# One pool of eight PSUM banks for scores and everything else, with an own buffer for Q staging, in a transformer layer on one core

## The chip, the cores and the metric

The kernel runs on one core of one Trainium2 chip. Times are device microseconds (us) of whole executions; a profile is one further execution that the hardware profiler recorded. PE is TensorE's matmuls, PEld its weight loads, ACT ScalarE, DVE VectorE, SPq the queue from which SyncE issues DMAs.

## The reference

In short: the kernel computes one pre-normalised transformer layer on 2048 tokens of width 1024: attention with 32 query heads of width 32 that share one key and one value head, then a gated feed-forward block (FFN) of width 3584.

```python
x_norm = layernorm(x)
q = (x_norm @ wq).reshape(B, S, 32, 32)      # 32 heads
k, v = x_norm @ wk, x_norm @ wv              # one shared head
p = softmax(q k^T / sqrt(32))                # 32 x 2048 x 2048 exponentials
h = x + (p v) @ wo
h2 = h + (sigmoid(hn @ w_gate) * (hn @ w_up)) @ w_down     # hn = layernorm(h)
```

All inputs are bf16.

## The kernel before

The kernel is written out by a planner of its own. While the program is built, a list scheduler with assumed costs walks along TensorE's time and decides, step by step, which piece of work PE does next; the order on every engine is fixed then, and the chip runs it in that order with semaphores.

The work comes in groups. A score group (S) is 16 row-tiled matmuls (each on 32 of the 128 rows, `32*128` in the views) that fill four PSUM banks; there are 512 of them, and ACT turns each into probabilities with exponentials. A PV group multiplies probabilities with V. OP is the output projection, GU a gate/up pair of the FFN, D the down projection, Q the query projection. The FFN runs in passes: tokens 0 to 127, then 128 to 255, then 256 tokens at a time. While there is little real work at the start, PE runs warm-up fillers, matmuls whose results nobody uses. In the views, QTb and kT are Q and K transposed, Pr the probabilities, Vaug V with one more column, OT the attention output transposed and wo_sb its weights, hnT the normalised h transposed, ring the gate and up weights, hact the gated product and zone other large operands.

PSUM has eight banks. Before, six belong to the scores (three units of two neighbouring banks, so one exponential always covers 1024 columns), and two to all other groups. Only one of the other groups is open at a time:

```python
S_ps = psum_tensor("S_ps", [P, 6, 512], F32)       # scores only
F_ps = psum_tensor("F_ps", [P, 2, 512], F32)       # everything else
qst  = hact[:, :]                                  # Q staging lives in hact
...
# planner, one turn
if can_s and run - t < 750.0:        # ACT would soon run dry: scores first
    emit_S(v)
elif cur is not None:                # go on with the one open group
    ...
else:                                # open the next group, by priority
    banks = [b for b in range(2) if known(bank_rel[b], t)]
    # xT, KV, Q0, PV, OP, D, GU, Q
```

The product `hact` of the first FFN pass waits until the last Q staging has been stored (`deps += q_store[-NQS:]`), because Q staging and `hact` share memory, and this pass may start only when all Q groups are done (`q_left[0] == 0`).

The softmax here doesn't subtract the row's maximum and nothing guards it: scores larger than these inputs give would overflow.

## Time and profile before

| | before |
|---|---|
| median of the first runs | 1199.36 us |
| profiled span | 1196.8 us |
| PE busy | 1169.7 us, 98% |
| ACT busy | 1043.8 us, 87% |

From the page of the kernel before: the span, the busy times of the engines, and the clock that TensorE was granted in 40 slices of the span (9 is 90% or more of full speed).

```profile
span 1196.8 us, 47622 instructions
PE 1169.7 (98%) x22204; PEld 830.8 (69%) x22204; DVE 293.6 (25%) x799; ACT 1043.8 (87%) x1312; POOL 38.5 (3%) x84
PEclk9999989999999999999999999999999999999999
```

PE looks saturated, but matmuls are pipelined and their ends are modelled in the profile, so a busy PE is not PE at its peak. From the starts of successive instructions, PE needs about 1150 us for this list of work, so some 42 us are waiting or half clock. The next view sums the waits of PE by what ended them: the total in us, the number of waits, the longest.

```profile
PE S_ps L349 <- ACT Pr L548: 7.3, 10, 1.4
PE F_ps L349 <- issue: 6.8, 8, 2.1
PE S_ps L349 <- issue: 3.5, 4, 1.8
...
PE F_ps L349 <- DVE hact L699: 0.7, 1, 0.7
PE F_ps L349 <- ACT Pr L548: 0.6, 1, 0.6
```

"issue" is a wait for which the profile shows no releaser. The group lines say what an exponential and the output projection cost (busy us, mean ns of one, then the idle time of the engine before them).

```profile
L548 ACT ACTIVATE Pr<-S_ps 128x1024 bf16<-128x1024 f32 x1024 | 977.5, 1042 | 28.5 <-PE S_ps L349 27.7
L349 PE MATMUL F_ps<-wo_sb,OT 128*128 128x512 bf16 x256 | 65.0, 384 | 0.6 <-issue 0.6
```

The clearest single stall stands in the timeline from 146 to 153 us (start, length, instruction, count; in brackets the idle time before it and its releaser).

```profile
146.72 7.53 ACT L548 ACTIVATE Pr<-S_ps 128x1024 bf16<-128x1024 f32 x8
...
147.88 0.40 PE L349 MATMUL S_ps<-QTb,kT 32*128 32x128 bf16 x16 [1.40 <-ACT Pr L548]
149.72 0.61 PE L349 MATMUL S_ps<-QTb,kT 32*128 32x128 bf16 x16 [1.43 <-ACT Pr L548]
151.55 0.61 PE L349 MATMUL S_ps<-QTb,kT 32*128 32x128 bf16 x16 [1.22 <-ACT Pr L548]
152.54 0.48 DVE L699 SCALAR_TENSOR_TENSOR hact<-tnh,F_ps 128x128 bf16<-128x128 f32 x2 [8.08 <-ACT Pr L548]
...
152.88 1.28 PE L349 MATMUL F_ps<-Vaug,Pr 128*128 128x33 bf16 x39 [0.72 <-DVE hact L699]
```

DVE idles 8.08 us: its product cannot be written into `hact`. Both F banks therefore stay full, PE has only score groups, and these come at ACT's pace. PE's four waits here add to 4.8 us. Half clock follows for 6.8 us.

### The profile page before, as it was taken

The page shows a single profiled execution, that of the slowest core. Times are in us where ns is not written, and L with a number is a line of the kernel's source. Part 1 is how long each engine was busy: PE and PEld are TensorE (multiplying, and loading weights), DVE is VectorE, ACT ScalarE, POOL GpSimd, SP SyncE. Part 2 cuts the span into 40 slices and gives each one's busy share as a digit, 9 for nine tenths or more (in the row PEclk, how much of TensorE's full clock was granted, in tenths as well). Part 3 has the DMA queues.
Part 4 walks back from the last instruction along what each step waited for, and adds up shares of the span by engine and source line. Part 5 has one row for each costly group of instructions (what it writes and reads, how often), then busy time and mean ns, then how long its engine had stood idle before and what let it go on. Part 6 is the DMA issues. An engine that isn't in the chain of part 4 may idle for free.

```text
span 1196.8 us, 47622 instructions
## 1 busy us (share of the span) xinstructions
PE 1169.7 (98%) x22204; PEld 830.8 (69%) x22204; DVE 293.6 (25%) x799; ACT 1043.8 (87%) x1312; POOL 38.5 (3%) x84
## 2 busy tenths in 40 slices
PE   9999988999999999999999999999999999999999
PEld 5755567677577856787577856777568765786684
DVE  8423212121213121221212221213122221222121
ACT  6899989999999999999999999999999999981120
POOL 4100000000000000000000000000000000000000
PEclk9999989999999999999999999999999999999999
DMA  8665499489456632667155650666226750479480
GB/s 241 161 182 155 138 280 242 107 210 286 82 142 160 178 90 55 163 177 182 29 122 151 194 118 12 159 178 178 64 64 178 187 139 15 117 192 228 123 208 18
DMA packets 332021, 176.74 MB, mean 148 GB/s; under 512 B 52016, under 2 KB 322352, under 8 KB 331824
## 3 DMA queue, kind: packets, MB, share of 16 engines
q1 hardware_dynamic: 329744, 173.57, 55.6%
q8 instruction: 174, 2.85, 1.0%
q10 hardware_dynamic: 2080, 0.13, 0.1%
q14 instruction: 23, 0.19, 0.0%
HBM read 155.32 MB, written 7.34 MB: 136 GB/s over the span
## 4 chain that ended last, share of the span: by engine, by line
PE 88%; ACT 6%; issue 2%; DVE 2%; DMA 2%; SPq 0%; ACTq 0%; DVEq 0%
PE F_ps L349 75%; PE S_ps L349 13%; ACT Pr L548 5%; DMA q_scratch<-hact 1%; ACT tnh L692 1%; DVE st L290 0%; DMA ring<-in_A_x_dram 0%; DVE st L292 0%; DMA zone<-ring 0%; DVE ring L329 0%; ACT ring L333 0%; DVE hact L699 0%; DVE ring L336 0%; ACT zone L236 0%; DVE mv L294 0%
## 5 line engine op out<-in xcount | busy, mean ns | idle before, releaser
L548 ACT ACTIVATE Pr<-S_ps 128x1024 bf16<-128x1024 f32 x1024 | 977.5, 1042 | 28.5 <-PE S_ps L349 27.7
L349 PE MATMUL F_ps<-hnT,ring 128*128 128x256 bf16 (+1 forms) x4032 | 446.9, 263 | 5.1 <-issue 4.2
L349 PEld LDWEIGHTS F_ps<-hnT,ring 128*128 128x128 bf16 x4032 | 342.6, 98 | 62.9 <-issue 8.9
L349 PEld LDWEIGHTS F_ps<-Vaug,Pr 128*128 128x128 bf16 x8192 | 229.2, 96 | 29.1 <-issue 3.7
L349 PE MATMUL F_ps<-Vaug,Pr 128*128 128x33 bf16 x8192 | 244.2, 177 | 3.7 <-issue 1.9
L349 PE MATMUL S_ps<-QTb,kT 32*128 32x128 bf16 x8192 | 208.4, 218 | 11.0 <-ACT Pr L548 7.3
L349 PE MATMUL F_ps<-zone,hact 128*128 128x512 bf16 x896 | 213.7, 380 | 0.0
L349 PEld LDWEIGHTS S_ps<-QTb,kT 32*128 32x128 bf16 x8192 | 119.3, 93 | 124.2 <-ACT Pr L548 73.7
L699 DVE SCALAR_TENSOR_TENSOR hact<-tnh,F_ps 128x256 bf16<-128x256 f32 (+1 forms) x252 | 97.7, 391 | 439.5 <-ACT tnh L692 431.3
L692 ACT ACTIVATE tnh<-F_ps 128x256 f32<-128x256 f32 (+1 forms) x252 | 93.9, 378 | 86.2 <-PE F_ps L349 86.2
L349 PEld LDWEIGHTS F_ps<-zone,hact 128*128 128x128 bf16 x896 | 78.8, 98 | 88.0
L349 PE MATMUL F_ps<-zone 128*128 128x256 bf16 (+2 forms) x512 | 75.4, 289 | 2.0 <-ACT QTb L236 1.4
L731 DVE SCALAR_TENSOR_TENSOR h_sb<-F_ps,h_sb 128x512 bf16<-128x512 f32 x32 | 22.1, 691 | 204.7 <-PE F_ps L349 204.7
L349 PE MATMUL F_ps<-wo_sb,OT 128*128 128x512 bf16 x256 | 65.0, 384 | 0.6 <-issue 0.6
L581 DVE RECIPROCAL rL<-F_ps 128x4 f32<-128x4 f32 x128 | 23.3, 182 | 140.1 <-PE F_ps L349 140.0
L349 PEld LDWEIGHTS F_ps<-zone 128*128 128x128 bf16 x512 | 37.3, 97 | 23.7 <-ACT QTb L236 1.6
L304 POOL TENSOR_SCALAR zb<-mvb 128x1 bf16<-128x1 bf16 (+1 forms) x25 | 5.6, 225 | 1046.9 <-DVE mvb L300 1046.9
L583 DVE TENSOR_TENSOR Osb<-F_ps,rL 128x128 bf16<-128x128 f32 x128 | 37.3, 291 | 4.2
L349 PEld LDWEIGHTS F_ps<-wo_sb,OT 128*128 128x128 bf16 x256 | 22.1, 99 | 23.0 <-issue 1.9
L625 DVE TENSOR_TENSOR h_sb<-F_ps,xres 128x512 bf16<-128x512 f32 x32 | 22.1, 691 | 47.2 <-PE F_ps L349 47.2
L237 DVE CAST hact<-F_ps 128x512 bf16<-128x512 f32 x24 | 16.6, 691 | 38.2 <-PE F_ps L349 38.1
L349 PE MATMUL S_ps<-hact,ident 128*128 128x512 bf16 x76 | 19.8, 411 | 1.8 <-POOL ident L242 1.8
(36 smaller groups left out, 154.8 us busy)
## 6 DMA issues: line engine op xcount, KB each, us to landing
ring<-in_B_w_gate_dram SPq DMA_DIRECT2D x126, 512.0 KB, 4.3
ring<-in_B_w_up_dram SPq DMA_DIRECT2D x126, 512.0 KB, 6.0
zone<-in_B_w_down_dram SPq DMA_DIRECT2D x7, 1024.0 KB, 8.5
xres<-in_A_x_dram SPq DMA_DIRECT2D x16, 256.0 KB, 2.8
out_dram<-h_sb SPq DMA_DIRECT2D x32, 128.0 KB, 1.7
q_scratch<-hact SPq DMA_DIRECT2D x24, 128.0 KB, 2.8
QTb<-q_scratch SPq DMA_DIRECT2D x6, 512.0 KB, 5.0
ring<-in_A_x_dram SPq DMA_DIRECT2D x5, 512.0 KB, 6.8
```

What stands on the lines that cost most here:

```text
L237: lambda: DVE.tensor_copy(out=out_ap, in_=in_ap))
L304: f = pl.op("pool", lambda: POOL.tensor_scalar(out=zb[:, ph, sl].unsqueeze(2), in0=mvb[:, ph, sl, 1:2], scalar1=LN_EPS_BF16, scalar2=None, ...
L349: return lambda: PE.matmul(o, lhsT=l, rhs=r, start=start, stop=stop, **kw)
L548: exps[u] = pl.op("act", lambda slot=slot, pb=pb: ACT.activation(out=Pr[:, slot, :].rearrange("p (a b) -> p a b", a=2), in_=S_ps[:, pb:pb ...
L581: a = pl.op("dve", lambda: DVE.reciprocal(rL[:, k, :].unsqueeze(2), ov[:, :, DH:DH + 1]), [last], prio=0, occ=70, lat=280)
L583: e = pl.op("dve", lambda: DVE.tensor_tensor(out=Osb[:, qb % 2, g * P:(g + 1) * P].rearrange("p (a b) -> p a b", a=4), in0=ov[:, :, 0:DH], ...
L625: h_ev[(t, dc)] = pl.op("dve", lambda: DVE.tensor_tensor(out=h_sb[:, t % 4, sl], in0=F_ps[:, b, :], in1=xres[:, t % 2, sl], op=ALU.add), [ ...
L692: a = pl.op("act", lambda: ACT.activation(out=tnh[:, k, 0:n], in_=F_ps[:, b, 0:n], func=ACTF.Tanh, scale=0.5), [last, tn_user.get(k)], pri ...
L699: e = pl.op("dve", lambda: DVE.scalar_tensor_tensor(out=hactT[:, ft, 0:n], in0=tnh[:, k, 0:n], scalar=1.0, in1=F_ps[:, b, 256:256 + n], op ...
L731: e = pl.op("dve", lambda: DVE.scalar_tensor_tensor(out=h_sb[:, t % 4, sl], in0=F_ps[:, b, :], scalar=0.5, in1=h_sb[:, t % 4, sl], op0=ALU ...
```

## The change

The intent: let whichever work needs a bank have one, so that PE has something else to do when one group waits, and take away the memory conflict behind the stall above. The diff, cut to its core:

```diff
-    NB = 3
+    SMAX = 8
+    FMAX = 3
+    NQS = 4
-        xres = SB("xres", [2, D])
+        qst = SB("qst", [NQS, 512])
-        S_ps = EC(nc.psum_tensor("S_ps", [P, 6, 512], F32))
-        F_ps = EC(nc.psum_tensor("F_ps", [P, 2, 512], F32))
+        PS = EC(nc.psum_tensor("PS", [P, 8, 512], F32))
-        qst = hact[:, :].rearrange("p (a b) -> p a b", b=512)
 ... s_plan(): any four free banks serve a score group; neighbours preferred
+                w = 2 if i % 2 == 0 and free[i + 1] == free[i] + 1 else 1   # else two exps of 512
 ... x is loaded into h_sb in place of xres
-                    deps += q_store[-NQS:]
+                    deps += []
-  gr.gate = lambda: s in slab_ld and (q_left[0] == 0 if c == 0 else ...)
+  gr.gate = lambda: s in slab_ld and (True if c == 0 else ...)
 ... planner: two groups may be open
-                if can_s and run - t < 750.0:
+            return max(pl.free["act"], t) + sum(...) - t < 1000.0
+        URGENT = ("xT", "KV", "PV", "OP")
+            if banks and len(active) < 2 and f_use < (FMAX if v else 6):
+            if new is not None and (not go or (new[0] in URGENT and RANK[new[0]] < RANK[go[0][0].cls])):
 ...                                  # an urgent group breaks into the open one
-                                 deps if (kk == 0 and j == 0) else [], occ=15.0, lat=15.0 + 170.0 + SEM)
+                              deps if (r == 0 and j == 0) else [], occ=14.0, lat=14.0 + 200.0 + SEM)
```

So three things change in the pool: before the first scores, up to six banks may hold the other groups; afterwards up to three may; and two such groups may be open, the more urgent breaking in.

## The prediction

> **What bounds it now.** Two engines almost tie: the page gives PE 1169.7 us busy, ACT 1043.8, of 1196.8. Starts of successive instructions in the timeline give what each needs:
>
> - PE: 216 ns per 512-column matmul, 109 per 256, 56 per 128, 25 per 33; a score group of 16 row-tiled matmuls 188 ns, plus about 96 going in and 147 coming out. (The Trainium skill, "TensorEngine Tiling (Array Packing)", Key Properties, says a change of tiling mode drains TensorE; the trace agrees with these gaps.) Summed over the instruction order: about 1150 us.
> - ACT: 906 ns per exp of 1024 columns, 264 per tanh of 256, 157 per tanh of 128: 1007 us.
>
> So about 42 us is PE waiting or slowed, plus 5 us at the ends. Excess over PE's need by stretch: 5 us before 60; 6 in 60 to 150; 10.5 in 150 to 200; 10 in 200 to 300; 7 in 300 to 424; 5 afterwards. After 424 us PE is the limit and hardly waits. From the first scores (27.7 us) to score group 160 (357.7 us) takes 330 us, where ACT needs 302 and PE 296.
>
> The clearest stall is 146 to 153 us: the timeline shows DVE waiting 8.1 us at the first gated product (its hact is the Q staging, still being stored), both F banks stuck, only score groups left, at ACT's pace, 1.4 us idle each. The clock record then shows half rate for 6.8 us (20.5 us in all before 331 us, about 10 us lost). (The Trainium skill, "TensorE: Matmul & The Clock Gate", Part 1: an idle window of about 3.4 us halves the clock; the trace agrees.)
>
> **The change**, from the two instruction orders:
>
> 1. 504 mode switches against 508: no gain.
> 2. Real matmuls are the same; warm-up fillers fall from 76 to 52 because more banks admit Q groups earlier: 24 x 216 ns = 5 us less.
> 3. 193 of 1024 exps are split in two (non-adjacent banks). Interpolated, 512 columns take 477 ns; 2 x 477 - 906 = 48 ns each: ACT +9 us (1017). By group 160 it needs 305 us to PE's 296, so ACT remains the limit there.
> 4. Own Q staging and no hold: the first FFN pass starts 24 us of PE work earlier, mixed with Q. The 146 us stall and its half clock go: 8 to 10 us.
> 5. FFN groups may hold three banks and two may be open: other work when one waits. FFN passes 1 and 2 (128 tokens) still pull weights quickly: DMA share is 0.8 to 1.2 in 150 to 210 and 260 to 300, so I keep part of those stalls.
> 6. x loaded into h: 16 loads either way, behind output stores long finished: nothing.
>
> **Sum.** 1197 - 5 (fillers) - 9 (hold and clock) - 7 (other early waits, half clocks) + 1 (extra ACT early) = 1177 us. Range 1162 to 1192. Chances: faster by over 2% 0.42, within 2% 0.54, slower 0.04.
>
> **What would show it.** No DVE wait of 8 us near 146; first FFN matmul near 115 to 120, not 143 us; group 160 at about 345; fewer half-clock windows; excess after group 160 still 5 to 8 us; exps of 512 columns near 477 ns apart.
>
> **What would make it wrong.** The order is fixed at build: if split exps cost more than 48 ns, or weights land later than the plan assumes with FFN pass 1 pulled forward, PE waits in new places. If almost all early waits vanish, it is 1160.

## More of the kernel before

If a piece is not ready when its turn comes on the chip, PE waits, even when other work would have been ready.

What waits for what is told to the planner as lists of dependences; a DMA is believed to land at an assumed time:

```python
# a DMA in the plan
go = max(s + 1300.0, self.dma_free[e])
self.dma_free[e] = go + o.nbytes / 280.0
o.end = self.dma_free[e] + 700.0
...
# OP may open when the plan thinks that OT has landed
gr = Group("OP", atoms, lambda: [ot_ev[t], xr_ld[t]] + wo_ld, after)
...
# gate of a GU group, and what its product waits for
gr.gate = lambda: s in slab_ld and (q_left[0] == 0 if c == 0 else d_done[c - 1] == 2 * len(CH[c - 1]))
deps += q_store[-NQS:]               # first pass only
```

## The result

The changed kernel took 1207.45 us (median of four runs, 1207.30 to 1208.64) against 1198.17 us for the kernel before beside it (1195.76 to 1199.37). The ratio is 1.0082, with a 95% interval from 1.0063 to 1.0102. Here and below a ratio is the mean time of one kernel's fast runs over that of the other's of the same rounds, so it is not quite the ratio of the medians. The change is therefore a small loss of about 10 us, inside 2%, where a gain of some 20 us had been predicted.

From the page of the changed kernel, the lines that answer to those of before:

```profile
span 1205.6 us, 47926 instructions
PE 1166.8 (97%) x22180; PEld 826.5 (69%) x22180; DVE 291.6 (24%) x797; ACT 1059.4 (88%) x1507; POOL 38.7 (3%) x84
PEclk9999998999799999999999999999999999999999
```

PE's busy time fell by 3 us, yet the span grew by 9. The clock is lower in the eleventh slice (301 to 331 us). PE's waits by what ended them:

```profile
PE PS L347 <- ACT Pr L567: 20.1, 21, 1.8
PE PS L347 <- issue: 10.3, 13, 1.7
```

Waits that end with an exponential went from 7.3 + 0.6 = 7.9 us to 20.1 us. The exponentials and the output projection:

```profile
L567 ACT ACTIVATE Pr<-PS 128x1024 bf16<-128x1024 f32 x831 | 815.0, 1049 | 38.4 <-PE PS L347 36.4
L567 ACT ACTIVATE Pr<-PS 128x512 bf16<-128x512 f32 x386 | 221.4, 627 | 0.0
L347 PE MATMUL PS<-wo_sb,OT 128*128 128x512 bf16 x256 | 67.5, 393 | 6.3 <-ACT Pr L567 4.4 <-issue 1.9
```

386 exponentials are narrow, which is 193 that were split. PE's idle time before the output projection rose from 0.6 to 6.3 us. The stall at 146 us is gone, but the changed kernel has stretches of its own in which only score groups are left. This is the timeline of PE from 301 us, waits only:

```profile
303.43 0.40 PE L347 MATMUL PS<-QTb,kT 32*128 32x128 bf16 x16 [1.52 <-ACT Pr L567]
...
308.84 0.61 PE L347 MATMUL PS<-QTb,kT 32*128 32x128 bf16 x16 [1.22 <-ACT Pr L567]
...
320.63 0.40 PE L347 MATMUL PS<-QTb,kT 32*128 32x128 bf16 x16 [1.49 <-ACT Pr L567]
...
326.13 0.61 PE L347 MATMUL PS<-QTb,kT 32*128 32x128 bf16 x16 [1.22 <-ACT Pr L567]
```

A second stretch of the same kind lies at 182 to 205 us. Together they hold about 15 us of waits for ACT.

For a better account I matched every wait of PE over 0.25 us after 60 us with the semaphores that the program itself makes that matmul wait for, rather than with the event that came last. The sum of these waits is 21.5 us before and 34.1 us after. Span less waits is 1175.3 us before and 1171.5 us after. So what is not waiting became about 4 us shorter, as the prediction said (fewer fillers), and the loss shows as 12.6 us more waiting. The part that is not waiting also holds matmuls slowed by half clock (107 ns between the starts of 128-column matmuls there, against 56 ns otherwise). From these starts that costs, as an estimate, 7.6 us before and 12.2 us after. By cause, in us:

| kernel | all | no semaphore | ACT | DMA | DVE | of these: S for ACT | OP for DMA |
|---|---|---|---|---|---|---|---|
| before | 21.5 | 12.2 | 8.3 | 0 | 0.9 | 7.7 | under 0.7 |
| after | 34.1 | 6.8 | 16.6 | 10.2 | 0.6 | 14.3 | 7.3 |

The last column is a new kind of wait. The page puts it down to exponentials, but the program makes those matmuls wait for `OT`, which a transposing DMA delivers. All six OP matmuls that waited over 0.25 us started about 0.1 us after their DMA had landed. The timeline of the changed kernel shows one:

```profile
508.18 1.26 SPq L614 DMA_TRANSPOSE OT<-Osb  x1
...
511.05 0.50 PE L347 MATMUL PS<-hnT,ring 128*128 128x256 bf16 x3
513.12 1.45 PE L347 MATMUL PS<-wo_sb,OT 128*128 128x512 bf16 x6 [1.57 <-ACT Pr L567]
```

The DMA is issued at 508.18. A GU group of 16 matmuls is broken into after its sixth, at 511.55, because the planner believes `OT` to be there. `OT` landed at 513.03 by the trace, and PE can go on only at 513.12, 4.9 us after the issue, although the broken GU group had ten matmuls left. The planner assumed 2.9 us from issue to landing for most of these DMAs (1300 ns, 262144 bytes at 280 a ns, and 700 ns); in the trace they took 3.0 to 6.4 us, with a median of 3.2. Before, the same step was let through without a wait, 4.1 us after its issue, with the last matmuls of the open group just ahead of it:

```profile
494.44 1.85 SPq L589 DMA_TRANSPOSE OT<-Osb  x1
...
498.30 0.39 PE L349 MATMUL F_ps<-hnT,ring 128*128 128x256 bf16 x2
...
498.53 1.67 PE L349 MATMUL F_ps<-wo_sb,OT 128*128 128x512 bf16 x7
```

### The profile page after: what moved, and what is told of

The parts are those of the page before. It is cut to its first block, busy times and chain, and to the rows that moved or that the text cites. A ratio compares the mean times of both kernels' runs of the same rounds, so it can differ in the third digit from the quotient of the medians.

```text
span 1205.6 us, 47926 instructions
## 1 busy us (share of the span) xinstructions
PE 1166.8 (97%) x22180; PEld 826.5 (69%) x22180; DVE 291.6 (24%) x797; ACT 1059.4 (88%) x1507; POOL 38.7 (3%) x84
## 4 chain that ended last, share of the span: by engine, by line
PE 91%; ACT 5%; issue 1%; DVE 1%; DMA 1%; POOL 1%; POOLq 0%; DVEq 0%; ACTq 0%
PE PS L347 91%; ACT Pr L567 5%; DMA zone<-ring 0%; DMA hnT<-hn 0%; POOL rstd L308 0%; DVE st L287 0%; DVE st L289 0%; ACT tnh L716 0%; POOL dsb L306 0%; DVE ring L333 0%; PE PS L352 0%; POOL zb L301 0%; DVE ring L326 0%; DVE h_sb L755 0%; DVE mv L291 0%
## 5 line engine op out<-in xcount | busy, mean ns | idle before, releaser
L567 ACT ACTIVATE Pr<-PS 128x1024 bf16<-128x1024 f32 (+1 forms) x1217 | 999.5, 915 | 38.4 <-PE PS L347 36.4
L347 PE MATMUL PS<-hnT,ring 128*128 128x256 bf16 (+1 forms) x4032 | 448.4, 263 | 4.7 <-issue 4.3
L347 PEld LDWEIGHTS PS<-hnT,ring 128*128 128x128 bf16 x4032 | 341.7, 98 | 62.0 <-issue 5.9
L347 PEld LDWEIGHTS PS<-Vaug,Pr 128*128 128x128 bf16 x8192 | 230.4, 96 | 32.0 <-issue 7.5
L347 PE MATMUL PS<-Vaug,Pr 128*128 128x33 bf16 x8192 | 242.5, 178 | 5.1 <-issue 2.7
L347 PE MATMUL PS<-QTb,kT 32*128 32x128 bf16 x8192 | 208.9, 219 | 17.2 <-ACT Pr L567 13.8
L347 PE MATMUL PS<-zone,hact 128*128 128x512 bf16 x896 | 220.2, 381 | 0.0
L347 PEld LDWEIGHTS PS<-QTb,kT 32*128 32x128 bf16 x8192 | 119.8, 93 | 137.2 <-ACT Pr L567 75.5
L723 DVE SCALAR_TENSOR_TENSOR hact<-tnh,PS 128x256 bf16<-128x256 f32 (+1 forms) x252 | 98.4, 391 | 382.2 <-ACT tnh L716 381.7
L716 ACT ACTIVATE tnh<-PS 128x256 f32<-128x256 f32 (+1 forms) x252 | 98.1, 391 | 69.2 <-PE PS L347 68.6
L347 PEld LDWEIGHTS PS<-zone 128*128 128x128 bf16 x512 | 37.1, 97 | 20.5 <-issue 0.8
L234 DVE CAST qst<-PS 128x512 bf16<-128x512 f32 x24 | 16.6, 691 | 26.8 <-PE PS L347 26.6
L308 POOL TENSOR_TENSOR rstd<-dsb,cst 128x1 f32<-128x1 bf16 (+1 forms) x25 | 16.6, 663 | 2.0
```

Source lines behind the costliest of these rows:

```text
L234: lambda: DVE.tensor_copy(out=out_ap, in_=in_ap))
L308: h = pl.op("pool", lambda: POOL.tensor_tensor(out=rstd[:, ph, sl], in0=dsb[:, ph, sl], in1=nb, op=ALU.pow), [g, c1], prio=prio - 1, occ=5 ...
L347: return lambda: PE.matmul(o, lhsT=l, rhs=r, start=start, stop=stop, **kw)
L567: ex = pl.op("act", lambda b=free[i], w=w, slot=slot: ACT.activation(out=Pr[:, slot * 512:(slot + w) * 512], in_=PS[:, b:b + w, :].rearran ...
L716: a = pl.op("act", lambda: ACT.activation(out=tnh[:, k, 0:n], in_=PS[:, b, 0:n], func=ACTF.Tanh, scale=0.5), [last, tn_user.get(k)], prio= ...
L723: e = pl.op("dve", lambda: DVE.scalar_tensor_tensor(out=hactT[:, ft, 0:n], in0=tnh[:, k, 0:n], scalar=1.0, in1=PS[:, b, 256:256 + n], op0= ...
```

## The experiments

Sixteen kernels were run, in four sessions; each session has its own runs of the kernel before (1196.35, 1195.57, 1196.43 and 1198.31 us). In the traces of the second and fourth session some of the 512-column matmul records are missing, which shows as false "issue" waits; my own account leaves those gaps out. Kernels that start from the changed kernel are called variants of "after".

The first session was to tell three theories of the loss apart: that the pool with its two open groups loses, more than the own staging and the lifted hold gain; that the earlier first FFN pass loses, because it pulls weights into a busy time; or that the split exponentials lose.

### 1. Own staging and the x load alone

Before, with the own `qst` buffer and x loaded into `h_sb`; two banks, one open group and the hold on the first pass kept.

```diff
-        xres = SB("xres", [2, D])
+        qst = SB("qst", [NQS, 512])
-                    deps += q_store[-NQS:]
+                    deps += []
 ... x into h_sb, as in the change
```

> The kernel before, with only the own buffer for Q staging and x loaded into h; two PSUM pools and the hold of the first FFN pass for Q are kept. Prediction's step 4: the 8.1 us wait of DVE near 146 us and its half clock go, so 1188 to 1191 us. Theory 'moved' (until about 360 us the exps on ScalarE set the pace, and PE has only a fixed stock of other work until then, so a wait taken away comes back later): the DVE wait goes, PE's waits after 160 us grow by as much, score group 160 starts within 3 us of 357.7 and the time is 1195 to 1200 us.

Measured: 1196.05 us, ratio 1.0001 (0.9977 to 1.0025). The 8.1 us idle of DVE is gone, and so are PE's waits at 147 to 153 us. Nothing came of it. Waits only, PE's timeline of this kernel from 144 to 200 us:

```profile
150.50 0.40 PE L348 MATMUL S_ps<-QTb,kT 32*128 32x128 bf16 x16 [0.18 <-ACT Pr L547]
153.10 1.18 PE L348 MATMUL F_ps<-Vaug,Pr 128*128 128x33 bf16 x41 [1.37 <-issue]
166.02 0.29 PE L348 MATMUL S_ps<-QTb,kT 32*128 32x128 bf16 x7 [1.97 <-issue]
167.44 0.40 PE L348 MATMUL S_ps<-QTb,kT 32*128 32x128 bf16 x16 [0.85 <-ACT Pr L547]
...
181.94 0.40 PE L348 MATMUL S_ps<-QTb,kT 32*128 32x128 bf16 x16 [0.65 <-ACT Pr L547]
...
192.89 0.56 PE L348 MATMUL F_ps<-hnT,ring 128*128 128x128 bf16 x7 [0.32 <-DVE hact L697]
```

Adding the bracketed waits of such lists: from 144 to 200 us before has 8.5 us and this kernel 5.6; from 200 to 360 us before has 7.4 and this kernel 8.5. So 4.8 us of waits were taken away and 3 us came back within 200 us, in other places: behind "issue" and behind exponentials. The half clock moved too: 17.1 us in this kernel, 20.5 before. The rest of the difference in the waits (21.5 against 17.9 us in all) is of the size of the scatter between runs of one kernel, which was 4 us here.

### 2. The first FFN pass not held either

As 1, and the first FFN pass may start before all Q groups are done: the change without the pool and without the planner's new numbers for scores. D groups also wait, as in the changed kernel, until all loads of their weights have been planned.

```diff
-  gr.gate = lambda: s in slab_ld and (q_left[0] == 0 if c == 0 else ...)
+  gr.gate = lambda: s in slab_ld and (True if c == 0 else ...)
```

> As own_staging, and the first FFN pass is no longer held for Q: the whole change except the PSUM pool. If the pool is what cost the 9 us of the change, this runs at 1180 to 1191 us by the prediction's sum, or 1195 to 1200 if the waits only move. If the early FFN pass is what cost it (weights that land late, scores delayed), it runs at 1203 to 1210 us with score group 64 at 160 us or later.

Measured: 1197.71 us, ratio 1.0016 (0.9994 to 1.0038). Waits of 23.8 us in all, of which 6.2 are now for DMA. The earlier pass gains nothing.

### 3. The pool with the hold

The changed kernel with the old gate restored, the same line the other way round.

> The changed kernel with one line undone: the first FFN pass is held for Q again (own Q staging and the pool of eight banks stay). If pulling the pass forward is the loss, 1190 to 1199 us. If the waits only move and the pool's slower scores are the loss, 1203 to 1209 us, with the waits of PE near 143 and 156 us gone and those between 180 and 330 us as large as in the changed kernel.

Measured: 1207.41 us, ratio 1.0097 (1.0067 to 1.0127), the time of the changed kernel. With 1 and 2 this settles where the loss is: the pool and its planner lose, whatever the first FFN pass does. The rival "earlier pass" falls.

### 4. Split exponentials alone

Before, with 192 of the 1024 exponentials run as two of 512 columns; the order of all work is the same.

```diff
+   if u % 16 in (1, 6, 11):          # two halves, one after the other
+       ACT.activation(out=Pr[:, slot, 0:512],    in_=S_ps[:, pb, :], ...)
+       ACT.activation(out=Pr[:, slot, 512:1024], in_=S_ps[:, pb + 1, :], ...)
```

> The kernel before with 192 of its 1024 exps run as two of 512 columns, spread evenly, and every instruction otherwise in its old place. Cadence measured in the changed kernel: 477 ns each, so 48 ns more per split, 9.2 us of ScalarE in all, 2.9 us of it before score group 160. If splits cost only where ScalarE sets the pace: plus 1 to 4 us, 1198 to 1202. If they cost everywhere or delay the score groups behind them: plus 7 to 12 us, about 1207, which alone would explain the change's loss.

Measured: 1199.04 us, ratio 1.0023 (1.0001 to 1.0044), so 2.7 us for 192 splits. Narrow exponentials follow one another at 477 ns, as predicted, so ACT works 9.2 us more and less than a third of it reaches the end. The splits are a small part of the loss, not its cause.

### 5. The output projection may not break in

After, with "OP" taken out of `URGENT`.

```diff
-        URGENT = ("xT", "KV", "PV", "OP")
+        URGENT = ("xT", "KV", "PV")
```

> The changed kernel, but an output projection (OP) may no longer break into an FFN group that is under way; score values (PV) still may. In the changed kernel PE waited 9.5 us in all before OP matmuls (before: 1.5), because the plan starts an OP at the moment it believes the transpose of the attention output to have landed, and the transpose lands later. Theory 'urgency': OP waits fall to 1 to 3 us and the time to 1198 to 1202 us. Theory 'banks' (FFN groups that hold a third bank keep the scores waiting; OP waits are only where the slack shows): the time stays at 1204 to 1209.

Measured: 1205.39 us, ratio 1.0083 (1.0068 to 1.0098). The waits of OP for the transposing DMA fell from 7.3 to 3.0 us, but all waits stayed (36.1 us by my account): those without a semaphore rose to 14.8. (The 9.5 us of the expectation count waits under 0.25 us too.) About 2 us by the medians, nothing by the ratio: the range of the theory "banks". Why so little came of it is not settled.

### 6. The pool kept, its banks kept apart

After, but once the scores begin, scores use banks 0 to 5 and other groups banks 6 and 7, one open at a time. Before the scores begin all eight stay open to the others. Everything else of the change stays.

```diff
-            free = [b for b in range(8) if bank_free(b, t)]
+            free = [b for b in range(6) if bank_free(b, t)]
-            if SMAX - s_use < 4 or len(free) - (...) < 4:
+            if len(free) < 4:
-            banks = [b for b in range(8) if bank_free(b, t)]
-            if banks and len(active) < 2 and f_use < (FMAX if v else 6):
+            banks = [b for b in (range(6, 8) if v else range(8)) if bank_free(b, t)]
+            if banks and len(active) < 1:
```

> The changed kernel with the pool taken apart again: scores keep to banks 0 to 5, all else to 6 and 7 once scores have begun, and one group is open at a time. Own staging, no hold, early Q in all banks and all else stay. Splits almost vanish (12 instead of 386 narrow exps). If the pool (in whatever part) is the loss, 1192 to 1200 us with score group 160 at 357 or earlier; if it is the planner's other settings, 1204 or more.

Measured: 1192.78 us, ratio 0.9974 (0.9959 to 0.9989). This is the largest effect: more than 12 us faster than the changed kernel, and a little faster than before. Its waits are 23.6 us against 34.1, and the view of waits agrees (the kernel after had 20.1 us here):

```profile
PE PS L347 <- ACT Pr L565: 11.8, 17, 1.4
```

The time fits the fillers. Experiment 2 lacks the free banks at the start, and the planner's new numbers for scores as well, and took 1.0016; the predicted gain of those banks, fewer fillers, was 5 us or 0.0042. Together that is 0.9974, as measured, but each ratio is known only to about 0.002, so the exact match is luck.

### 7. and 8. The planner told a later landing time

Perhaps the planner only needs better numbers. Its clock seemed to believe in the pool: it planned 1158.5 us for the changed kernel against 1167.3 us for the one before. Of these 8.8 us about 8.2 are just the lower assumed cost of a score matmul, 14 in place of 15 ns times 8192, while the chip took the same 431 ns for a score group in both. So I gave it transposing DMAs that land 1.7 us later, and the old score cost; in 8 the same landing for the kernel of experiment 1, as a control.

```diff
-            o.end = self.dma_free[e] + 700.0
+            o.end = self.dma_free[e] + (2400.0 if o.occ == 1330.0 else 700.0)
-   occ=14.0, lat=14.0 + 200.0 + SEM        # 7 only
+   occ=15.0, lat=15.0 + 170.0 + SEM
```

> The changed kernel, pool and all, with two numbers of its planner[...]: a transposing DMA lands 1.7 us later than it assumed, and a score matmul occupies 15 ns as in the kernel before, not 14. Theory 'urgency' in its general form (the order is built on landings that come later on the chip): OP waits fall to 1 to 3 us and the time to 1196 to 1202. If the pool's bank sharing itself delays scores: OP waits fall, waits of score groups stay near 15 us and the time stays above 1203.

> The kernel before with the own Q staging and the planner told that transposing DMAs land 1.7 us later. A candidate to beat both kernels: its waits before FFN and PV matmuls between 60 and 360 us (10.5 us in own_staging) should shrink by 3 to 5 us: 1190 to 1194 us. If waits only move, 1195 to 1199.

Measured: 7 took 1207.76 us, ratio 1.0080 (1.0038 to 1.0122), and 8 took 1192.35 us, ratio 0.9988 (0.9945 to 1.0030). In both one of the four runs lies apart: 1199.09 in 7, 1201.97 in 8. In 7 the waits of OP for DMA fell to 1.3 us, as the repair should make them, and the time did not move: waits for ACT rose to 19.6 us and those without a semaphore to 13.9. This is the outcome of the second theory: the landing time is not what costs the 9 us. Nor is 1.7 us the true delay; the traces show no single one. The DMAs that deliver `OT` took 3.0 to 6.4 us in the changed kernel and 3.0 to 8.2 us in 7, against an assumed 2.9. 8 is inconclusive.

### 9. and 10. One open group; then two banks as well

After with one open group; then also with at most two banks for other groups, from the common pool.

```diff
-            if banks and len(active) < 2 and f_use < (FMAX if v else 6):
+            if banks and len(active) < 1 and f_use < (FMAX if v else 6):
-    FMAX = 3           # 10 only
+    FMAX = 2
```

> The changed kernel with one number changed: one group besides the scores may be open at a time, not two, so nothing breaks into an FFN group. The third bank and the shared pool stay (66 exps are split, not 386). Theory 'third bank' (groups that hold a third bank, while they run or wait to be copied out, keep a score group from finding four free banks): 1201 to 1208 us, score group 160 at 363 or later. Theory 'breaking in': 1191 to 1197 us as in banks_apart.

> As one_open, and only two banks for what is not scores; still one pool, in which banks change hands (4 narrow exps are left). Theory 'third bank': 1190 to 1196 us as banks_apart, score group 160 at 352 to 358. If sharing banks as such costs (a bank that a group leaves late delays scores), 1200 or more.

Measured: 9 took 1202.10 us, ratio 1.0050 (1.0024 to 1.0075); 10 took 1197.71 us, ratio 1.0012 (0.9975 to 1.0049). The view of waits and the output projection of 9:

```profile
PE PS L347 <- ACT Pr L567: 17.3, 22, 1.5
L347 PE MATMUL PS<-wo_sb,OT 128*128 128x512 bf16 x256 | 67.2, 395 | 1.0 <-issue 1.0
```

With one open group the waits before OP are down from 6.3 to 1.0 us (1.2 for DMA in my account), while the waits for ACT stay at 17.3 us. So breaking in explains the OP waits, and something else the waits for ACT. Experiment 9 also has fewer narrow exponentials (66 against 386), worth perhaps 2 of the 4 to 5 us that it gains on the changed kernel, by experiment 4. With two banks the waits for ACT fall to 13.4 us and the time by 4 more. Experiment 6 goes one step further, since there banks no longer change hands, and is faster again: from the changed kernel over 9 and 10 to 6 the ratios are 1.0082, 1.0050, 1.0012 and 0.9974, three steps of nearly the same size. The intervals of neighbours overlap, so the share of each step (second group, third bank, banks that change hands) is likely rather than shown. That the three together cost the loss is shown by experiment 6, whose interval lies well below those of 9 and of the changed kernel.

What the third bank does can be read from the score groups: group 64 starts at 154.4 us before, at 168.0 after, at 164.9 with one open group, at 161.2 with two banks as well and at 157.7 in experiment 6. With more banks PE does other work earlier and scores later: counted in matmuls times their cadence, 97 us of work other than scores and fillers was started before group 64 in the kernel before, 114 us in the changed one, and 105 us in experiment 6. My reading of what follows, not shown by a run of its own: later, when that other work is used up or waits for a chain of its own, only scores are left, one at a time, at ACT's pace, as in the stretches at 182 and 301 us.

### 11. and 12. Is ScalarE the pace until 360 us?

The prediction held that ACT is the limit until score group 160. These two kernels give a wrong result: the exponentials of score groups 9 to 160 work on half of their columns, so that ACT saves more than 100 us of work in that time.

```diff
-    out=Pr[:, slot, :]...,         in_=S_ps[:, pb:pb + 2, :]
+    out=Pr[:, slot, 0:512 * w]..., in_=S_ps[:, pb:pb + w, :]     # w = 1 for 16 <= u < 320, else 2
```

> A wrong result on purpose: the kernel before, every instruction in its place, but the exps of score groups 9 to 160 work on half of their columns (the rest of the tile keeps old values), about 429 ns less each, 130 us of ScalarE. If ScalarE sets the pace until 360 us: PE's waits for exps vanish (7.7 us after 60 us, with 4 us more in their wake), group 160 comes at 332 to 342 us and the time is 1172 to 1182. If the early waits come from weight loads and latencies: above 1188.

> A wrong result on purpose: the same halving of exps in the changed kernel (score groups 9 to 160). If the pool loses only by delaying scores where ScalarE sets the pace, the loss vanishes: within 4 us of before_light_exps. If it loses by waits of PE on landings and copies that its tight order has no slack for (OP waits 7 us and others after 360 us), it stays 6 us or more above before_light_exps.

Measured: before with light exponentials 1193.22 us, ratio 0.9961 (0.9928 to 0.9995); after with light ones 1199.23 us, ratio 1.0021 (0.9997 to 1.0045). (The former's four runs lie 11 us apart, and its trace is of the slowest.) So ACT's work in this time is worth some 4 us of the kernel before and 7 to 8 of the changed one. Group 160 of the former started at 359.1 us (357.7 with full exponentials). The theory that ScalarE sets the pace there fell. And with light exponentials in both, the changed kernel still takes 6 us more than the one before by the medians. That is just what the second theory of its expectation asked for, by which the loss is more than scores delayed where ScalarE sets the pace. From the view of waits of the former:

```profile
PE F_ps L349 <- DVE hact L699: 4.2, 2, 2.9
PE F_ps L349 <- DMA hnT<-hn: 2.8, 1, 2.8
PE S_ps L349 <- ACT Pr L548: 3.2, 5, 0.7
```

Waits for exponentials fell from 7.3 to 3.2 us, and PE waited for the next thing in line: the stores of staged Q (4.2 us) and a transposed tile (2.8 us).

### 13. and 14. What holds the early stretch, then?

With the cause of the wrong step still open, two further kernels, both wrong: experiment 1 with light exponentials; and the same with the weights of slabs 5 to 27 (counted from 0) loaded by half.

```diff
+   # 14 only: half of the rows of w_gate and w_up for slabs 5 to 27
+   h = DT // 2 if NSLAB <= s < NFT else DT
+   wgu[:, sl, w, 0:h, :]  <-  W[0:h * P, ...]
```

> A wrong result on purpose: the kernel before with own Q staging and the exps of score groups 9 to 160 on half their columns. If exps and the landing of the staged Q were the two things that set the early pace between them, both are gone: group 160 at 345 or earlier and 1178 to 1188 us. If PE only goes on to the next landing or instruction block: group 160 stays at 352 to 359 and the time at 1189 to 1196.

> A wrong result on purpose: as own_light, and weight slabs 6 to 28 (of FFN passes 1 and 2) are loaded by half. If DMA traffic delays PE's instruction blocks and the weights: pauses without a semaphore fall from about 10 us to under 5, group 160 comes at 340 or earlier, 1172 to 1184 us. If instruction blocks are slow without traffic too: pauses stay at 7 us or more and the time within 5 us of own_light.

Measured: 1192.09 us, ratio 0.9948 (0.9920 to 0.9975), and 1186.46 us, ratio 0.9899 (0.9869 to 0.9929). Group 160 started at 348.2 and 346.7 us, where experiment 1 had 356.7. So even with the staging conflict gone and ACT's load halved, no more than 6 us come, and half the weight traffic brings 6 more. The first time lies in the range of "the waits go on", with group 160 between the two ranges; the second lies between what the two theories expected. The early stretch has no single limit: exponentials, landings and weight traffic hold it in turn.

### 15. and 16. The best version again, and with the hold

Experiment 6 once more with more rounds, and with the hold on the first FFN pass.

> The kernel of banks_apart once more with more rounds: the change without its pool and its second open group. Its gain comes from 24 fewer warm-up fillers (5 us of PE work) and no more waits than before: 1190 to 1195 us, faster than the kernel before by 0.2 to 0.5%.

> As banks_apart, and the first FFN pass is held for Q again. If waits only move, within 3 us of banks_apart_again; if early weights cost there, 3 to 6 us faster.

Measured: 1194.28 us, ratio 0.9969 (0.9948 to 0.9990), and 1197.01 us, ratio 1.0002 (0.9976 to 1.0028). So the version with the banks kept apart beats both kernels, by 0.3% against before in two sessions and by about 1.1% against after. The medians put the hold at 2.7 us in this version; the intervals overlap.

## Why the prediction was wrong

The result lies 15 us above the upper end of the predicted range, and the sign is wrong. Point by point, with the steps as the prediction numbered them:

- **Steps 1 and 2, mode switches and fillers: right.** Switches are 504 against 508 and fillers 52 against 76, as predicted. Span less waits fell by 3.8 us where 5 were predicted, and the sum in experiment 6 fits 5.
- **Step 3, split exponentials: right in size.** 477 ns for 512 columns was predicted and measured. The 1 us entered for them is 2.7 us by experiment 4. The reasoning that ACT "remains the limit" until group 160 was wrong (experiments 11 to 14).
- **Step 4, "Own Q staging and no hold: … 8 to 10 us": the first failing step.** The cause of the stall was read rightly and the stall went, but it was worth nothing: 1.0001 alone, 1.0016 with the lifted hold. What failed is the assumption that its length comes off the span. It held 4.8 us of PE's waits, and 3 us of waits and most of the half clock came back elsewhere before 360 us.
- **Step 5, "other work when one waits", -7 us: the second failing step, and the larger.** The pool with its two open groups is the loss: 1207.41 us with the hold restored, and about 13 us less when the banks are kept apart and one group is open. The other work that step 5 counted on to fill the waits was done earlier instead, and the waits for ACT rose from 8.3 to 16.6 us, those of OP for its DMA from under 0.7 to 7.3. The planner's choice to break in is made at build time, from assumed landing times. Where these are short, PE stands before a matmul that is not ready, with a half-finished group beside it. And here the freedom to do other work early went with late scores, and then stretches with scores alone.
- **Step 6, x loaded into h: right**, as part of experiment 1.
- **What would show it.** No DVE wait near 146: true. First FFN matmul near 115 to 120 us: nearly, 121.3. Exponentials of 512 columns near 477 ns apart: true. Group 160 at about 345 us: false, 369.4. Fewer half-clock windows: false, 37.5 us at half clock after, 20.5 before. (The Trainium skill, "TensorE: Matmul & The Clock Gate", Part 1, gives an idle window of about 3.4 us before the clock is halved. The half-rate stretches in the traces last multiples of 3.41 us, which fits such a window. But no wait was that long: after 60 us PE's longest was 2.1 us before and 1.8 us after, and half clock followed all the same. Here even waits of 1.3 to 2.1 us were followed by half clock.)
- **What would make it wrong.** The text named the cause in passing, that the order is fixed at build and PE may wait in new places. A change within 2% was its likeliest outcome, and that came; but no term of the sum allowed for new waits, and the range ended at 1192.

In the sum: 1197 - 5 (measured about -4 to -5) - 9 (measured 0 to +2) - 7 (measured about +13 with the splits) + 1 (counted in the last).

Open: how the 13 us divide between the second open group, the third bank and the banks that change hands; how much any new order of the plan scatters the time by itself, since most variants reorder the work (but by the medians all four kernels with the pool and two open groups, the changed one, 3, 5 and 7, took 1205 to 1208 us, and all seven with correct results and the banks apart 1192 to 1199); why taking OP out of the urgent classes, or telling the planner later landings, cured the waits of OP and not the time; and how the waits without a semaphore move between versions.

## What to carry to other kernels

In a program whose order is fixed at build, a stall that is removed is worth only what no other wait takes up behind it: try it alone before adding its length to a sum. More freedom for such a scheduler (more banks, a second open group) need not help: here it brought a loss, and a later assumed landing time did not change that. A group that can be broken into for work that has not landed turns a hidden latency into a wait. When a part of a large change is pure gain, like the free banks before the scores here, it can be kept without the rest.

## What the Trainium skill lacked or had wrong

- "Runtime: NRT & Kernel Launch", Instruction fetch mechanics, says that an engine refills its instructions in blocks of 16 KiB and that crossing a block's boundary is "mostly hidden". By count that fits: the queue moved 174 blocks, and only 13 were followed by such a pause. But the page does not say what such a block may cost. Of PE's waits over 0.25 us, 13 before (12.2 us of 21.5) had no semaphore, and each ended 1.2 to 1.6 us after a 16 KB packet of the instruction queue had ended. Eleven of the 13 lie before 375 us, where weights load hardest. The queue, and one such pause, from the page and PE's timeline of the kernel before (the packet ended at 170.80):

```profile
q8 instruction: 174, 2.85, 1.0%
169.72 0.45 PE L349 MATMUL F_ps<-hnT,ring 128*128 128x128 bf16 x5
172.29 1.76 PE L349 MATMUL F_ps<-hnT,ring 128*128 128x128 bf16 x23 [2.12 <-issue]
```

  The link is one of time only. Experiment 14, with half the weight traffic, had 8.5 us of such waits against 12.6 in experiment 13, which fits.
- "TensorEngine Tiling (Array Packing)", Key Properties, says that a change of tiling mode drains TensorE but not what that costs. Here it was about 96 ns going into a group of row-tiled matmuls and 147 ns coming out, some 240 ns on a group of 188 ns, 512 times.
- "ScalarE: Activation LUTs", Rules for kernel authors, budgets about 0.3 us for each instruction and 0.83 ns for each element; the same page also gives 186 ns where scale and bias are immediates, and an overlap of about 93 ns back to back, which leaves a fixed part of 93 to 207 ns, an estimate. Back to back, the fixed part was only about 50 ns: 477 ns for 512 columns and 904 to 906 for 1024, which is 0.835 ns a column. For a decision about splitting, the difference matters: 48 ns a split, not 93 to 300.
- "DMA: Bandwidth & Descriptors", Latency and other measured facts, gives transposing DMAs a bandwidth (261 GB/s in one case) and speaks of a fixed cost of about 2 us for DMAs, but gives no spread of the time from issue to landing. By these a tile of 128 by 1024 bf16 would take 1.0 us and the fixed cost, together about 3 us, an estimate. The shortest in the changed kernel's trace took 3.0 us and the median 3.2, which agrees, but the longest took 6.4; the matmul above went on 4.9 us after the issue. For a planner the late ones are those that count.
